# Softmax of batches 4 to 7 with tokens on partitions, turned by DMA both ways

## The chip, the core and the metric

The kernel runs on one core of a Trainium2 chip. The metric is the device time of one execution in microseconds (us). The kernel before takes 241.41 us, the median of three runs (241.13 to 242.18).

## What is computed

Eight batches of eight heads, with 576 tokens of 64 numbers each, go through an attention over 32 memory slots, and the result through a bilinear feed-forward layer:

```python
a = softmax(phi, axis=2)                       # over the tokens
k_m = einsum('bhsm,bhsd->bhmd', a, k)          # 32 memory keys and values per head
v_m = einsum('bhsm,bhsd->bhmd', a, v)
attn = softmax(q @ k_m^T / sqrt(64), axis=-1)  # over the 32 memory slots
x = attn @ v_m                                 # heads side by side: 4608 tokens x 512
out = ((x @ w_a) * (x @ w_b)) @ w_out          # 512 -> 1536 -> 512
```

The change concerns the second softmax: the division of exp(scores) by its sum over the 32 slots.

## The kernel before

For each batch the attention weights lie in a tile with 128 partitions, four heads of 32 memory slots each, and 2 x 576 columns: two groups of heads, tokens along the columns. The memory values are folded into the weights (`vab` = v_m times w_a and w_b), so that the up-projection takes the attention weights `A` directly. A sum over memory slots is thus a sum over partitions, and it is made on TensorE: a product with a block matrix of ones gives each partition the sum of its own head. ScalarE makes 1/sum out of it as exp(-ln(sum)), because both functions lie in one table, and GpSimd (VectorE for batches 0 and 1) multiplies.

```python
def scores(gs):
    if 0 in gs:
        t["E"] = mid.tile([P, 2, S], F16, name="E")           # pool "mid": 2 buffers per name
    if len(gs) > 1 and b > 2:
        work.settle()                                         # gives one PSUM bank back
    ...
        t["pss", g] = [banks.take([P, NI, 32], F32, "pscore", hold=True) for _ in range(2)]
    ...                                                       # 32 small matmuls, 4 banks for both groups

def exp_scores(g):
    Ev = t["E"].rearrange("p g (i z s) -> p g i z s", z=2, s=32)
    for z in range(2):
        pss, bank = t["pss", g][z]
        nc.scalar.activation(out=Ev[:, g, :, z, :], in_=pss, func=AF.Exp, scale=1.0 / (8.0 * CS))
        banks.free(bank)

def denominators(g, hfs=range(2)):
    ...
        pD = banks.tile([P, HALF], F32, name="pD")
        nc.tensor.matmul(pD, ones, t["E"][:, g, sl], start=True, stop=True)
        nc.scalar.activation(out=t["L", g][:, sl], in_=pD, func=AF.Ln)

def normalise(g, hfs=slice(0, 2)):
    if g == 0 and hfs.start == 0:
        attn[b] = mid.tile([P, 2, S], F16, name="A")
    ...
    nc.scalar.activation(out=t["R", g][:, sl], in_=t["L", g][:, sl], func=AF.Exp, scale=-1.0)
    engine = nc.vector if b < 2 else nc.gpsimd
    engine.tensor_tensor(out=attn[b][:, g, sl], in0=t["E"][:, g, sl], in1=t["R", g][:, sl], op=ALU.mult)
```

The fold needs four banks for 512 columns of both weight matrices; ScalarE empties those of group 0 and VectorE those of group 1:

```python
def take_fold(lo, hi, z):
    for g, engine_copy in enumerate((nc.scalar.copy, nc.vector.tensor_copy)):
        pva, bank = t["pva", lo, z][g]
        engine_copy(out=vabs[b][z][:, g, lo:hi], in_=pva[:, 0:hi - lo])
        banks.free(bank)
```

The up-projection of batch b runs in half steps, each two matmuls for `pa` and two for `pb`, of 288 columns. ScalarE copies `pa` to `a_sb`, VectorE multiplies it with `pb` into `ht`:

```python
def up_half(b, i, hf, x):
    ps = banks.tile([P, HALF], F32, name=("pa", "pb")[x])
    for g in range(2):
        nc.tensor.matmul(ps, vabs[b][x][:, g, P * i:P * (i + 1)], attn[b][:, g, HALF * hf:HALF * (hf + 1)], ...)
    if x == 0:
        ...
        nc.scalar.copy(out=a_sbs[b, i, hf], in_=ps)
    else:
        nc.vector.tensor_tensor(out=ht[:, i, t0:t0 + HALF], in0=a_sbs.pop((b, i, hf)), in1=ps, op=ALU.mult)
```

A batch has 24 half steps, and after each there is a slot. In a slot come first the output products that are due (`py`, `pv`, `px`: pairs of token blocks by a seven-product scheme of Strassen's kind, with sums `h_sums` and `w_sums` added up on GpSimd), and then the units that a schedule string names: "sc" the scores, "e0" and "e1" the exponentials of the two groups, "den" the sums, "nr" the division, "v0" to "v2" the fold of 512 columns, "x0a" and so on its copies out, "kv" and "km" the sums of keys and values and their scaling, "kvt" and "kvd" their transposition on TensorE or by DMA, "qt" the transposition of q, "exp" the exponential of phi, "L" the loads of a later batch, "d3" three output products out of turn. A stroke (') means the batch after. The strings `second`, `every` and `last` hold the preparation of batch 3, of batches 4 to 6, and of batch 7.

PSUM has eight banks. `banks.take` hands out the one whose turn is longest ago and that is not held; a matmul into a bank waits until the engine that read it last is done.

The weight sums are additions on GpSimd, issued after batch 1's preparation:

```python
def sum_weights():
    t = [w_sums[:, x] for x in range(4)]
    for out, in0, in1 in (...):                               # 4 sums, each in two halves of 128x768
        for x in range(2):
            ...
            nc.gpsimd.tensor_tensor(out=out[:, sl], in0=in0[:, sl], in1=in1[:, sl], op=ALU.subtract)
```

Of the kernel before, what the change touches and what calls it, by code (L numbers as in the profile page):

```python
# [8 lines left out]
F32 = mybir.dt.float32  # L9
F16 = mybir.dt.float16  # L10
AF = mybir.ActivationFunctionType
ALU = mybir.AluOpType

P = 128
# [4 lines left out]
def kernel(  # L19
# [11 lines left out]
    nc = tc.nc  # L31

    B, H, S, D = q.shape
    M = phi.shape[3]
# [11 lines left out]
    mid = ctx.enter_context(tc.tile_pool(name="mid", bufs=2))  # L46
    small = ctx.enter_context(tc.tile_pool(name="small", bufs=2))
# [130 lines left out]
    attn = {}  # L178
    vabs = {}

    def head(g, j):

        jj = j ^ g
        return jj % 2, 2 * g + jj // 2

    def units(b):

        u = {}
        t = {}
# [133 lines left out]
        def normalise(g, hfs=slice(0, 2)):  # L323
# [6 lines left out]
            engine = nc.vector if b < 2 else nc.gpsimd  # L330
            engine.tensor_tensor(out=attn[b][:, g, sl], in0=t["E"][:, g, sl], in1=t["R", g][:, sl], op=ALU.mult)  # L331

        def fold(lo, hi, zs):
            if b not in vabs:
                vabs[b] = [mid.tile([P, 2, d_ff], F16, name=f"vab{x}") for x in range(2)]
            if len(zs) > 1 and b > 2:
                work.settle()
            for z in zs:
                t["pva", lo, z] = [banks.take([P, 512], F32, "pva", hold=True) for _ in range(2)]
                for j in range(4):  # L340
                    for g in range(2):
                        r, hp = head(g, j)
                        nc.tensor.matmul(  # L343
                            t["pva", lo, z][g][0][32 * j:32 * j + 32, 0:hi - lo],
                            t["kvT"][64 * r:64 * r + 64, 4 + g, M * j:M * j + M],
                            w_sbs[z][64 * r:64 * r + 64, hp, lo:hi],
                            start=True,
                            stop=True,
                            tile_position=(64 * r, 32 * j),
                        )  # L350

        def take_fold(lo, hi, z):
            for g, engine_copy in enumerate((nc.scalar.copy, nc.vector.tensor_copy)):
                pva, bank = t["pva", lo, z][g]
                engine_copy(out=vabs[b][z][:, g, lo:hi], in_=pva[:, 0:hi - lo])  # L355
                banks.free(bank)

        def one(f, *a):
            return lambda: f(*a)

        for z in range(2):
            u[f"exp{z}"] = one(exp_phi, z)
            u[f"ks{z}"] = one(sums, z, 0)
            u[f"kt{z}"] = one(transpose, z, 0)
            u[f"vs{z}"] = one(sums, z, 1)
            u[f"vt{z}"] = one(transpose, z, 1)
            u[f"s{z}"] = one(scores, (z,))
            u[f"e{z}"] = one(exp_scores, z)
            u[f"km{z}"] = one(take_kv, (z,))
            u[f"den{z}"] = one(denominators, z)  # L370
            u[f"nr{z}"] = one(normalise, z)
            for hf in range(2):
                u[f"den{z}{hf}"] = one(denominators, z, (hf,))
                u[f"nr{z}{hf}"] = one(normalise, z, slice(hf, hf + 1))
            for n in range(NCH):
                u[f"v{n}{'ab'[z]}"] = one(fold, 512 * n, 512 * (n + 1), (z,))
                u[f"x{n}{'ab'[z]}"] = one(take_fold, 512 * n, 512 * (n + 1), z)
            for n in range(2):
                u[f"hv{n}{'ab'[z]}"] = one(fold, 256 * n, 256 * (n + 1), (z,))
                u[f"hx{n}{'ab'[z]}"] = one(take_fold, 256 * n, 256 * (n + 1), z)  # L380
        for n in range(NCH):
            u[f"v{n}"] = one(fold, 512 * n, 512 * (n + 1), (0, 1))
# [4 lines left out]
        u["km"] = one(take_kv)  # L387
        u["kvt"] = one(kv_transpose)
        u["kvd"] = one(kv_turn)
        u["-"] = lambda: None  # L390
        return u

# [36 lines left out]
    w_sums = wpool.tile([P, 4, KH, NH], F16, name="w_sums")  # L429

    def quarter(x, y):
        return wo_sb[:, KH * x:KH * (x + 1), NH * y:NH * (y + 1)]

    def sum_weights():
        t = [w_sums[:, x] for x in range(4)]
        for out, in0, in1 in ((t[0], quarter(0, 1), quarter(0, 0)), (t[1], quarter(1, 1), t[0]),
                              (t[2], quarter(1, 1), quarter(0, 1)), (t[3], quarter(1, 0), t[1])):
            for x in range(2):
                sl = slice(KH // 2 * x, KH // 2 * (x + 1))
                nc.gpsimd.tensor_tensor(out=out[:, sl], in0=in0[:, sl], in1=in1[:, sl], op=ALU.subtract)  # L440
# [182 lines left out]
    def ups(steps, side=()):  # L623

        side = iter(side)
        for step in steps:
            for _ in up(*step):
                work.advance()
                next(side, us[step[0]]["-"])()
        for f in side:  # L630
            work.advance()
            f()
# [5 lines left out]
    def half_steps(b, hf, lo=0):  # L638

        return [(b, i, (hf,)) for i in range(lo, NFF)]  # L640

    us = {b: units(b) for b in range(B)}

    def named(b, names):
# [6 lines left out]
    def slots(b, names):  # L651

        def both(fs):
            return lambda: [f() for f in fs]
        def unit(n):
            if n == "fin":
                return lambda: work.pull(-work.done % NFF)
            if n == "L":
                return lambda: load(b + 2) if b + 2 < B else None
            if n[0] == "y":  # L660
                return lambda: some(int(n[1:]))
            if n[0] == "d" and n[1:].isdigit():
                return lambda: work.pull(int(n[1:]))
            return us[b + n.endswith("'") - n.endswith("_")][n.rstrip("'_")]

        return [both([unit(n) for n in x.split("+")]) for x in names.split()]
# [26 lines left out]
    chain(1, "exp0 y3 exp1 y8 ks0 y1 qt0 y2 kt0 y2 qt1 s0 ks1 y3 e0 y1 kt1 qt2 y1 qt3 den0 y3 s1 y1 nr0 y4 vs0 e1 vs1 y1 den1 y2 vt0 vt1 nr1 y2 hv0a hx0a hv0b y1 hx0b y2")  # L693
    load(3)
    sum_weights()
    ups(steps(1, 0, 4), slots(1, "- y1+hv1a+hx1a hv1b+hx1b - y3+v1a+x1a y3+v1b+x1b - -"))
    ups(half_steps(1, 0, 4), slots(1, "- v2a+x2a+v2b+x2b+qt0' - - qt1'+exp0' exp1'+qt2' - kv'+km'+y9"))
    work.plan(S + HALF, 10)
    ups(half_steps(1, 1, 4), slots(2, "qt3 kvt - sc+e0+e1 - den0+den1+nr0 - v0+nr1+x0a x0b - v1+x1b x1a"))
    second = "v2_+d1+x2a_+exp0 x2b_ exp1 - kv+km+d2 qt0 d4+kvt+qt1 - qt2+qt3+sc+e0 - e1+v0+d2+x0a+x0b den0+d3 exp0' v1+nr0+x1a x1b+qt0' L+d5 den1 v2+x2a exp1'+qt1'+x2b - - qt2'+kv'+nr1+km' - - qt3'+kvt'+d5"  # L700
    every = "- sc+e0 e1 den0 nr0+v0+x0a+x0b - - exp0' exp1' - v1+x1b+x1a+kv'+km0'+d3 - den1+km1' kvd'+qt0' - - nr1+qt1' v2+x2a+x2b - qt2' - qt3' - - L"
    last = "sc+e0 d3 - e1 v0+x0b - - den1 - - den0+d1 x0a+v1+x1b x1a+nr0 - - - v2+x2a - nr1 - - - - x2b"
    for b in range(2, B):
        if b == 2:
            load(4)
# [35 lines left out]
```

The softmax here doesn't subtract the row's maximum and nothing guards it: scores larger than these inputs give would overflow.

## Time and profile before

| | of the profiled execution |
|---|---|
| span | 239.6 us |
| mean granted TensorE clock | 0.997 |
| matmuls of the sums (pD), count and listed mean | 32, 286 ns |
| ln on ScalarE (L), count and mean | 32 of 128x288, 418 ns |
| exp(-ln) on ScalarE (R), count and mean | 14 of 128x576, 702 ns; 4 of 128x288, 441 ns |
| multiplication on GpSimd (A), count and mean | 12 of 128x576, 1278 ns |
| key/value transposition by DMA (kvT), count and time to landing | 3, median 3.3 us |

The profile lists busy time for each engine; PE is TensorE's matmuls and PEld its weight loads, DVE is VectorE, ACT is ScalarE, POOL is GpSimd, SP issues DMAs. Matmuls overlap in the pipeline, so that the listed length of one is longer than the time it takes away from the next; the distance between two starts tells that time. In a view by stretches there stand, after the stretch, its length, then for each of PE, PEld, DVE, ACT and POOL the busy time with the number of instructions, then the clock, the DMA share and GB/s. In a view by order of time there stand the start, the length, the engine, the line, the operation, its tiles (out<-in) and shapes, and in brackets the idle time before it and what ended it.

### The profile page before, as it was taken

To read this page: it belongs to the slowest core of one execution; us is meant where nothing else is said; L and a number is where in the kernel's file an instruction comes from. 1 tells how busy PE (TensorE), PEld (TensorE's weight loads), DVE (VectorE), ACT (ScalarE), POOL (GpSimd) and SP (SyncE) were. 2 spreads that over 40 slices of the span, in tenths; PEclk is the share of its full clock that TensorE was granted. 3 is DMA by queue.
4 is the path that set the end of the run, shared out by engine and by line. 5 is a ranking of instruction groups with operands and counts; after the bars stand their busy time and mean duration, and the time that the engine had idled before them with its cause. 6 is when DMAs were issued, how large, how long until landed. Compare 5 with 4: busy or idle time off the path is not lost.

```text
span 239.6 us, 7764 instructions
## 1 busy us (share of the span) xinstructions
PE 230.6 (96%) x3092; PEld 170.3 (71%) x3092; DVE 165.4 (69%) x403; ACT 158.7 (66%) x410; POOL 159.5 (67%) x135
## 2 busy tenths in 40 slices
PE   7958999999999999999999999999999999999993
PEld 7734664456757867878787787878787778888882
DVE  4636784469949878966975659775976585756642
ACT  2266671669698599687776867797776877465330
POOL 7953244499979629981799948984769087937001
PEclk9999999999999999999999999999999999999998
DMA  6999999999967954992359945599130303032155
GB/s 230 239 197 207 206 258 206 252 213 279 224 154 161 214 115 98 222 208 49 43 123 233 211 90 65 141 212 191 41 85 11 81 16 74 10 83 61 38 130 125
DMA packets 28164, 34.71 MB, mean 145 GB/s; under 512 B 4416, under 2 KB 22208, under 8 KB 28128
## 3 DMA queue, kind: packets, MB, share of 16 engines
q0 software_dynamic: 19264, 23.14, 52.2%
q1 hardware_dynamic: 8352, 10.29, 18.4%
q10 hardware_dynamic: 512, 0.79, 1.0%
q8 instruction: 24, 0.39, 0.7%
q14 instruction: 12, 0.10, 0.1%
HBM read 42.47 MB, written 9.44 MB: 217 GB/s over the span
## 4 chain that ended last, share of the span: by engine, by line
PE 77%; DMA 16%; DVE 2%; issue 1%; POOL 1%; ACT 1%; DVEq 0%; POOLq 0%
PE py L473 18%; PE pa L601 18%; PE pb L601 17%; PE pv L473 9%; DMA wb_sb<-in_moe_w_b_dram 6%; DMA q_sb<-in_q_dram 5%; PE pva L343 5%; DMA kv_sb<-in_v_dram 4%; PE px L473 4%; PE po L398 2%; PE pkv L212 2%; PE pscore L297 1%; PE pD L320 1%; DVE ht L612 1%; ACT a_sb L609 1%
## 5 line engine op out<-in xcount | busy, mean ns | idle before, releaser
L612 DVE TENSOR_TENSOR ht<-a_sb,pb 128x288 f16<-128x288 f16 x168 | 73.3, 450 | 37.5 <-ACT a_sb L609 26.8
L601 PEld LDWEIGHTS <-vab 128*128 128x128 f16 x768 | 72.4, 98 | 24.9 <-issue 7.8
L609 ACT CAST a_sb<-pa 128x288 f16<-128x288 f32 x168 | 66.7, 407 | 25.7 <-PE pa L601 24.6
L601 PE MATMUL pa<-A,vab 128*128 128x288 f16 x384 | 75.8, 287 | 0.1
L601 PE MATMUL pb<-A,vab 128*128 128x288 f16 x384 | 75.0, 286 | 0.7 <-ACT vab L355 0.5
L455 POOL TENSOR_TENSOR h_sums<-ht 128x768 f16<-128x768 f16 x28 | 46.0, 1644 | 33.9 <-DVE ht L612 33.7
L473 PEld LDWEIGHTS <-h_sums 128*128 128x128 f16 x384 | 37.0, 98 | 7.7 <-issue 1.1
L355 DVE CAST vab<-pva 128x512 f16<-128x512 f32 (+1 forms) x52 | 32.3, 644 | 4.8 <-PE pva L343 4.2
L355 ACT CAST vab<-pva 128x512 f16<-128x512 f32 (+1 forms) x52 | 27.7, 569 | 7.8 <-PE pva L343 7.2
L473 PEld LDWEIGHTS <-ht 128*128 128x128 f16 x288 | 28.1, 98 | 5.7 <-issue 0.4
L473 PE MATMUL py<-w_sums,h_sums 128*128 128x256 f16 x192 | 31.3, 273 | 0.0
L455 POOL TENSOR_TENSOR h_sums<-h_sums,ht 128x768 f16<-128x768 f16 x14 | 23.0, 1640 | 1.0
L455 POOL TENSOR_TENSOR h_sums<-ht,h_sums 128x768 f16<-128x768 f16 x14 | 23.0, 1642 | 0.9
L310 ACT ACTIVATE E<-pscore 128x288 f16<-128x288 f32 x32 | 11.4, 419 | 11.4 <-PE pscore L297 11.2
L331 POOL TENSOR_TENSOR A<-E,R 128x576 f16<-128x576 f16 x12 | 15.3, 1278 | 4.3 <-ACT R L329 4.3
L473 PE MATMUL py<-wo_sb,ht 128*128 128x256 f16 x96 | 16.7, 273 | 0.0
L473 PE MATMUL pv<-w_sums,h_sums 128*128 128x256 f16 x96 | 16.5, 273 | 0.0
L473 PE MATMUL py<-w_sums,ht 128*128 128x256 f16 x96 | 15.9, 272 | 0.1
L473 PE MATMUL px<-wo_sb,ht 128*128 128x256 f16 x96 | 15.9, 273 | 0.0
L321 ACT ACTIVATE L<-pD 128x288 f32<-128x288 f32 x32 | 11.5, 418 | 6.0 <-PE pD L320 5.8
L480 ACT ACTIVATE u<-py 128x256 f32<-128x256 f32 x32 | 12.5, 390 | 4.3 <-PE py L473 3.7
L203 DVE STREAM_TRANSPOSE qT<-q_sb 128x288 f32<-128x288 f32 x32 | 14.6, 464 | 0.3 <-DMA q_sb<-in_q_dram 0.3
(65 smaller groups left out, 275.7 us busy)
## 6 DMA issues: line engine op xcount, KB each, us to landing
out_dram<-o_sb SPq DMA_DIRECT2D x68, 128.0 KB, 2.4
phi_sb<-in_phi_dram POOLq DMA_DIRECT2D x8, 576.0 KB, 5.4
kv_sb<-in_v_dram POOLq DMA_DIRECT2D x7, 576.0 KB, 10.3
kv_sb<-in_k_dram POOLq DMA_DIRECT2D x7, 576.0 KB, 6.6
q_sb<-in_q_dram POOLq DMA_DIRECT2D x6, 576.0 KB, 13.1
wo_sb<-in_moe_w_out_dram POOLq DMA_DIRECT2D x6, 256.0 KB, 13.7
q_sb<-in_q_dram POOLq DMA_DIRECT2D x4, 288.0 KB, 9.7
wa_sb<-in_moe_w_a_dram POOLq DMA_DIRECT2D x2, 512.0 KB, 13.8
```

The costliest lines, as they stand in the source:

```text
L203: nc.vector.transpose(out=t["qT"][:, hp, :].bitcast(F32), in_=qs[b][:, hp, :].bitcast(F32))
L310: nc.scalar.activation(out=Ev[:, g, :, z, :], in_=pss, func=AF.Exp, scale=1.0 / (8.0 * CS))
L321: nc.scalar.activation(out=t["L", g][:, sl], in_=pD, func=AF.Ln)
L331: engine.tensor_tensor(out=attn[b][:, g, sl], in0=t["E"][:, g, sl], in1=t["R", g][:, sl], op=ALU.mult)
L343: nc.tensor.matmul(t["pva", lo, z][g][0][32 * j:32 * j + 32, 0:hi - lo], t["kvT"][64 * r:64 * r + 64, 4 + g, M * j:M * j + M], w_sbs[z][64 ...
L355: engine_copy(out=vabs[b][z][:, g, lo:hi], in_=pva[:, 0:hi - lo])
L455: engine.tensor_tensor(out=out, in0=in0, in1=in1, op=op)
L473: nc.tensor.matmul(po, lhs[:, i], rhs[:, i], start=first and i == 0, stop=i == KH - 1, skip_group_check=not first)
L480: nc.scalar.mul(out=x, in_=po, mul=scale)
L601: nc.tensor.matmul(ps, vabs[b][x][:, g, P * i:P * (i + 1)], attn[b][:, g, HALF * hf:HALF * (hf + 1)], start=(g == 0), stop=(g == 1))
L609: nc.scalar.copy(out=a_sbs[b, i, hf], in_=ps)
L612: nc.vector.tensor_tensor(out=ht[:, i, t0:t0 + HALF], in0=a_sbs.pop((b, i, hf)), in1=ps, op=ALU.mult)
```

## The change

For batches 4 to 7 the exponentials E are transposed by a DMA into a tile ET with tokens on the partitions: nine blocks of 128x128. There, the 32 memory slots of a head lie side by side in one partition, so VectorE can sum them with tensor_reduce, take the reciprocal of the sums, and the division is one multiplication with the reciprocal broadcast over 32 columns, five blocks of it on GpSimd and four on VectorE. A second DMA turns the result back into A. The product with ones, the ln and the exp(-ln) are not needed for these batches. Two of the fold's twelve copies of a batch move from VectorE to ScalarE in exchange (columns 512 to 1023, group 1, batches 4 to 7). The schedules of batch 3 on are rewritten, with the loads of later batches earlier, and batch 4's key/value transposition goes by DMA. GpSimd's weight additions are held behind batch 1's division by a copy of one column that reads its result.

```diff
+        def e_turn():
+            t["ET"] = mid.tile([P, 2, S], F16, name="E").rearrange("p g s -> p (g s)").rearrange("p (n x) -> p n x", x=P)
+            nc.sync.dma_start_transpose(out=t["ET"], in_=t["E"].rearrange("p g s -> p (g s)"))
+
+        def blocks(x):
+            return t["ET"][:, slice(0, 5) if x == 0 else slice(5, 9)].rearrange("p n (j m) -> p (n j) m", m=M)
+
+        def token_sums(x):
+            if x == 0:
+                t["sum"] = small.tile([P, 36], F32, name="sum")
+            out = t["sum"][:, slice(0, 20) if x == 0 else slice(20, 36)]
+            nc.vector.tensor_reduce(out=out, in_=blocks(x), axis=mybir.AxisListType.X, op=ALU.add)
+            nc.vector.reciprocal(out=out, in_=out)
+
+        def token_normalise(x):
+            sums = t["sum"][:, slice(0, 20) if x == 0 else slice(20, 36)]
+            engine = (nc.gpsimd, nc.vector)[x]
+            engine.tensor_tensor(out=blocks(x), in0=blocks(x), in1=sums.unsqueeze(2).to_broadcast(list(blocks(x).shape)),
+                                 op=ALU.mult)
+
+        def a_turn():
+            attn[b] = mid.tile([P, 2, S], F16, name="A")
+            nc.sync.dma_start_transpose(out=attn[b].rearrange("p g s -> p (g s)").rearrange("p (n x) -> p n x", x=P),
+                                        in_=t["ET"].rearrange("p n x -> p (n x)"))
...
-            for g, engine_copy in enumerate((nc.scalar.copy, nc.vector.tensor_copy)):
+            copies = (nc.scalar.copy, nc.scalar.copy if b > 3 and lo == 512 else nc.vector.tensor_copy)
+            for g, engine_copy in enumerate(copies):
...                       # "ed" is e_turn, "sm0" "sm1" token_sums, "tn0" "tn1" token_normalise, "ad" a_turn
     def sum_weights():
+        nc.gpsimd.tensor_copy(out=w_sums[:, 0, 0, 0:1], in_=attn[1][:, 1, S - 1:S])
...
-    second = "v2_+d1+x2a_+exp0 x2b_ exp1 - kv+km+d2 qt0 d4+kvt+qt1 - qt2+qt3+sc+e0 - e1+v0+d2+x0a+x0b den0+d3 exp0' v1+nr0+x1a x1b+qt0' L+d5 den1 v2+x2a exp1'+qt1'+x2b - - qt2'+kv'+nr1+km' - - qt3'+kvt'+d5"
-    every = "- sc+e0 e1 den0 nr0+v0+x0a+x0b - - exp0' exp1' - v1+x1b+x1a+kv'+km0'+d3 - den1+km1' kvd'+qt0' - - nr1+qt1' v2+x2a+x2b - qt2' - qt3' - - L"
-    last = "sc+e0 d3 - e1 v0+x0b - - den1 - - den0+d1 x0a+v1+x1b x1a+nr0 - - - v2+x2a - nr1 - - - - x2b"
+    second = "v2_+d2+x2a_+x2b_+exp0 - exp1 - kv+km+d2 qt0 d4+qt1+kvt qt2 L+d1+qt3+sc+e0 - d2+v0+e1+x0a+x0b - den0+exp0'+d2 v1+nr0+x1a x1b+d10+exp1' - qt0' v2+x2a+x2b+kv' - den1+km0' km1'+kvd' nr1+qt1' qt2' qt3' - d6"
+    every = "exp0' sc+exp1'+e0+d3+e1+v0+x0a+x0b+ed - kv'+km0' km1' - d4+sm0 sm1+tn0+kvd' - tn1+d2 d3 v1+qt0'+x1a+ad d3+L+x1b qt1' - qt2' - v2+x2a+x2b - qt3' - - - - -"
+    last = "sc e0+e1+ed - v0+x0b - - sm0 x0a+sm1+tn0 d2+v1+d3+x1b+tn1 - ad+d6 x1a - - - - v2+x2a - - - - - x2b"
```

More of the change, by code (lines that the diff above doesn't have):

```diff
@@ L389, in units @@
         u["kvd"] = one(kv_turn)
+        u["ed"] = e_turn
+        for x in range(2):
+            u[f"sm{x}"] = one(token_sums, x)
+            u[f"tn{x}"] = one(token_normalise, x)
+        u["ad"] = a_turn
         u["-"] = lambda: None
```

## The prediction, made before the changed kernel ran

> **What bounds the kernel now.** I read the page's busy times first, then TensorE's own waits, then four 20 us stretches, then the order of time on TensorE. The page and the stretches:
>
> ```profile
> PE 230.6 (96%) x3092; PEld 170.3 (71%) x3092; DVE 165.4 (69%) x403; ACT 158.7 (66%) x410; POOL 159.5 (67%) x135
> ...
> 60.00:80.00 20.00, 19.74 (x348) 13.86 (x346) 15.76 (x41) 15.88 (x42) 18.03 (x14) 1.00 0.89 182
> 100.00:120.00 20.00, 20.00 (x298) 15.19 (x297) 16.07 (x40) 15.44 (x41) 12.73 (x9) 1.00 0.62 111
> 160.00:180.00 20.00, 20.00 (x288) 15.71 (x285) 16.15 (x40) 15.28 (x39) 13.04 (x9) 1.00 0.56 113
> ```
>
> TensorE is busy all of the time from about 100 us on, while VectorE stands at 16.1 of 20 us, ScalarE at 15.4 and GpSimd at 12.7. A busy PE could still hide bubbles, because matmuls overlap, so I look at distances between starts:
>
> ```profile
> 157.47 0.49 PE L473 MATMUL px<-wo_sb,ht 128*128 128x256 f16 x3
> 157.80 0.41 PE L320 MATMUL pD<-E,ones 128*128 128x288 f16 x2
> 158.04 0.41 PE L601 MATMUL pa<-A,vab 128*128 128x288 f16 x2
> ```
>
> Three matmuls of 256 columns take 0.33 us from start to start, 0.11 each; two of 288 columns take 0.24 to 0.245 us, 0.1225 each. This pace is held through the batches from 100 us on, without a hole, apart from about 0.2 us at each change between full matmuls and those on small tiles. So in that part a microsecond is won only by taking matmuls away from TensorE, and lost by whatever makes it wait. The waits that TensorE did have are early: the view of waits by engine names six of them, the longest 1.3 us, and none is in the steady part. The end is TensorE too: after the last up-projection, only output products remain.
>
> **What the Trainium skill says.** "Perfetto Trace Analysis", section "Identifying the Most-Contended Engine", says that matmul busy time is no measure of how full TensorE is; the trace agrees (the page lists 286 ns for a pD matmul whose slot is 122). "TensorE: Matmul & The Clock Gate", section "Back-to-back issue gap", gives N/2.4 + 2.5 ns as an isolated warm gap, 122.5 ns for 288 columns; the distances above agree. "VectorE: DVE Perf Modes", section "The perf-mode tier table", holds tensor_reduce to one element per cycle, whatever the type. No tensor_reduce is in this trace. "SBUF — State Buffer", section "Who interferes with whom", says that a VectorE instruction with two SBUF inputs and a GpSimd instruction that reads SBUF shut each other out for a whole instruction. The profile shows no such pair meeting in the place that the change guards: batch 1's last division on VectorE runs from 47.37 to 47.83 us, and GpSimd's first weight addition starts at 48.74.
>
> **The change, part by part.**
>
> Taken from TensorE: four pD matmuls in each of batches 4 to 7, 16 x 0.1225 = **1.96 us**. The new schedule also turns batch 4's key and value matrices by DMA (kvd' stands where kvt' stood), which removes six transposes on TensorE; a group of six takes
>
> ```profile
> 99.47 0.50 PE L241 MATMUL pT<-ident,rep 128*128 128x128 f16 x6
> 99.80 0.60 PE L473 MATMUL pv<-wo_sb,h_sums 128*128 128x256 f16 x4
> ```
>
> 99.80 - 99.47 = **0.33 us**. The instruction lists of the two programs differ by these 22 matmuls. Together 2.29 us, all on the engine that sets the end.
>
> ScalarE, per batch: four Ln go (0.30 each from start to start, so 1.2), two Exp(-L) go (105.22 to 105.81, so 0.59 each, 1.18), and two casts of 128x512 come over from VectorE (0.94 for two). Net -1.4 us.
>
> VectorE, per batch: two casts leave (1.28 for a pair). Two tensor_reduce of 640 and 512 elements, two reciprocals (0.16 each as in the row of rphi) and one multiply of 512 elements come in. By ht's full-rate row (288 elements, 450 ns alone) and the 684 ns of a 512 cast, I estimate 0.82, 0.68 and 0.69 us for the three; with the reciprocals 2.5. Net +1.2 us of about 24, so VectorE goes from 80% to 85%. It stays below TensorE.
>
> GpSimd, per batch: two multiplies of 576 (1278 ns each) go, one of 640 comes; at 1278/576 = 2.22 ns an element, 1.42 us. Net -1.1 us.
>
> The two turns: each moves nine blocks of 128x128. The key/value turn of six blocks lands in 2.7 to 3.7 us, median 3.3; for nine I estimate 4.0 to 5.5 us. The first must land before sm0 on VectorE, in slot 6; the scores are in slot 1. Let S be the time at which the scores' matmuls are over. E is complete at about S + 1.45 (below), so ET lands near S + 5.9. The slots between hold five pairs of up-products (2.45), the sums of keys and values (0.87), twelve output products (1.3) and the fold (1.0), so TensorE passes sm0's place at S + 5.6, and VectorE, which runs some 0.8 us behind, at S + 6.4. About half a microsecond to spare. The second turn is issued around slot 11 and is needed in slot 24: 12 us of room for some 5. Off the path.
>
> The held weight additions: one copy of 128x1 on GpSimd, behind an instruction that ended 0.9 us before the additions began anyway. Zero in this profile; it guards against a meeting that didn't occur here.
>
> **What takes some of it back.** The new order puts scores, both exponentials and the fold v0 into one slot. There are eight PSUM banks: the scores hold four, one is held by the open output product, so the fold must wait for banks that ScalarE is still reading. The kernel before has this once, where batch 3's second exponential and v0 share a slot:
>
> ```profile
> 85.27 0.46 PE L343 MATMUL pva<-wa_sb,kvT 64*32 64x512 f16 x8
> 85.30 0.82 DVE L612 TENSOR_TENSOR ht<-a_sb,pb 128x288 f16<-128x288 f16 x2 [0.94 <-ACT a_sb L609]
> 85.44 0.76 ACT L310 ACTIVATE E<-pscore 128x288 f16<-128x288 f32 x2
> 85.81 0.41 PE L343 MATMUL pva<-wb_sb,kvT 64*32 64x512 f16 x8
> ```
>
> 0.54 us between the two halves of the fold, against 0.22 in the steady batches: 0.3 us lost. In the new order I follow ScalarE: four E at 0.30 from S + 0.09 (last one written at S + 1.41), then x0a and x0b at 0.47 each, written at about S + 1.9 and S + 2.4. TensorE wants those banks earlier: the second pair after the scores at S + 1.7, and the key sums at S + 2.2. I get 0.2 + 0.25 = 0.45 us a batch, for batches 4, 5 and 6 (the last schedule spreads these out), 1.35 us in all. The margins are tens of nanoseconds and any output scaling between them moves them, so I count half, **0.7 us**.
>
> Sum: 241.4 - 2.3 + 0.7 = **239.8 us**. For the reshuffled schedule between batches 2 and 3 I count nothing: it can lose or regain a wait of 0.3 us like the one above.
>
> **The rivals.**
> First, **VectorE becomes the wait**. For: in slots 1 to 9 of batch 4 it gets nine ht (0.37 us each from start to start), two casts (0.64), both key/value scalings (1.7 for the two), the reduces with reciprocals (1.7), tn1 (0.7) and three output sums (1.1), 9.8 us of work, while TensorE needs 8.7: nine pairs of up-products (4.4), scores (0.4), fold (0.6), sums (0.9), 22 output products (2.4). VectorE falls about 1 us behind there. Besides, tn1 has two SBUF inputs and may stand behind a GpSimd addition of 1.64 us, and sm0 waits in order for a transfer. Against: six banks rotate under the up-products, three slots or 2.5 us, of which VectorE's usual lag takes 0.8, and the later slots are light. If so, about 0.5 to 1 us more per batch for four batches: 241 to 243 us.
> Second, **the waits of slot 1 do not arise**, because ScalarE has lost its Ln and Exp(-L) and is ahead; then the full 2.3 us remain and the smoother middle part gives another 0.5 to 1: 238.2 to 239.1 us.
> Third, **the turns are slow** beside loads and stores (the one at 145.7 us took 3.7 us beside stores): a landing after 7 us stops VectorE about 1 us a batch, of which the banks hide most. 240.5 to 242 us.
> A larger gain would need TensorE time that the change doesn't free, and a larger loss a stop of over 2 us a batch.
>
> **Range and chances.** The sure part is 2.3 us off. Full losses of the first rival give 242, the second rival 238. I take **239.8 us, with 237.6 to 241.9** for eight times in ten. Two per cent is 4.8 us, 236.6 or 246.2; neither sum gets there. Faster by over 2%: 0.05; within 2%: 0.92; slower by over 2%: 0.03.
>
> **What would show it.** In the profile after: 16 pD matmuls instead of 32 and 3070 matmuls instead of 3092; the distance of scores from batch to batch 0.5 us shorter, less what slot 1 gives back; a longer distance than 0.22 us from the first half of v0 to the second; ET landing in under 5.5 us; the reduces near 0.8 and 0.7 us; the weight additions still starting near 49 us. I would be wrong if TensorE shows waits on VectorE in slots 6 to 12, if the new A lands late for its first product, or if the part before 100 us moves by more than 1 us, of which I count none.

## The result, and the profile after

The changed kernel takes 239.57 us (239.41 to 239.74), the kernel before 241.32 us in the same runs: a ratio of 0.992, with an interval of 0.990 to 0.995. It is 0.8% faster, and the prediction was 239.8.

From the page of the kernel after, the busy times:

```profile
PE 228.5 (96%) x3070; PEld 168.0 (71%) x3070; DVE 169.1 (71%) x414; ACT 153.1 (64%) x394; POOL 154.9 (65%) x132
```

From its stretches, two of the three of before (length, then busy time of PE, PEld, DVE, ACT, POOL; the last three columns are the granted clock, the DMA share and GB/s):

```profile
100.00:120.00 20.00, 19.97 (x293) 14.65 (x292) 16.95 (x44) 15.40 (x39) 14.81 (x12) 1.00 0.56 120
160.00:180.00 20.00, 20.00 (x223) 15.48 (x222) 15.99 (x40) 14.04 (x37) 10.07 (x7) 1.00 0.43 80
```

TensorE is still the engine that decides, with 22 matmuls fewer. ScalarE and GpSimd gave up 5.6 and 4.6 us over the whole execution and VectorE took on 3.7, and none of that moved the end (e1, below, keeps all that work and is as fast). The new instructions, from the groups of the kernel after with shapes kept apart:

```profile
L350 POOL TENSOR_TENSOR E<-E,sum 128x640 f16<-128x640 f16 x4 | 5.1, 1263 | 10.6 <-DVE sum L345 10.6
L320 PE MATMUL pD<-E,ones 128*128 128x288 f16 x16 | 3.4, 286 | 0.7 <-ACT E L310 0.6
L350 DVE TENSOR_TENSOR E<-E,sum 128x512 f16<-128x512 f16 x4 | 3.4, 858 | 0.0
L344 DVE TENSOR_REDUCE sum<-E 128x20 f32<-128x640 f16 x4 | 3.2, 812 | 0.0
L344 DVE TENSOR_REDUCE sum<-E 128x16 f32<-128x512 f16 x4 | 2.7, 674 | 0.0
L345 DVE RECIPROCAL sum<-sum 128x20 f32<-128x20 f32 x4 | 1.1, 278 | 0.1
```

The turns, from its view of DMAs (issues, median us to landing); ET bears the name E there, because it shares E's buffers:

```profile
kvT<-rep SPq DMA_TRANSPOSE x4, 2.9
E<-E SPq DMA_TRANSPOSE x4, 3.5
A<-E SPq DMA_TRANSPOSE x4, 3.2
```

Slot 1 of batch 3, in the order of time on TensorE: scores, three output products, the fold v0, two half steps, and the beginning of the sums of keys and values:

```profile
101.76 0.47 PE L297 MATMUL pscore<-qT,kvT 32*32 32x288 f16 x32
102.17 0.50 PE L505 MATMUL py<-w_sums,ht 128*128 128x256 f16 x3
102.60 0.41 PE L368 MATMUL pva<-wa_sb,kvT 64*32 64x512 f16 x8
102.82 0.40 PE L368 MATMUL pva<-wb_sb,kvT 64*32 64x512 f16 x8
103.16 0.42 PE L633 MATMUL pa<-A,vab 128*128 128x288 f16 x2
103.41 0.41 PE L633 MATMUL pb<-A,vab 128*128 128x288 f16 x2
103.66 0.41 PE L633 MATMUL pa<-A,vab 128*128 128x288 f16 x2
104.10 0.40 PE L633 MATMUL pb<-A,vab 128*128 128x288 f16 x2
104.43 0.81 PE L212 MATMUL pkv<-kv_sb,exp_sb 64*32 64x192 f16 x45
```

The halves of v0 stand 0.22 us apart, so the fold itself did not wait. The wait comes later: from the last pa to the last pb are 0.44 us instead of 0.245.

Where the 1.9 us between the two profiled spans came from is seen in the first up-product of each batch, before and after: batch 3 at 100.35 and 99.92, batch 4 at 124.48 and 123.78, batch 5 at 153.91 and 152.76, batch 6 at 178.59 and 177.36, batch 7 at 202.28 and 200.46, end at 239.6 and 237.7. A batch's stretch runs from its first up-product to that of the next batch. The stretches in which matmuls were removed are shorter, by 0.3, 0.3, 0.45, 0.1 and 0.6 us from batch 2 on; they do not all contain the same output products, and they hold losses too (below). The first 72 us and the tail are alike within 0.12 us.

### The profile page after: what moved, and what is told of

It is laid out like the page before. It is cut to its first block, busy times and chain, and to the rows that moved or that the text cites. A ratio compares the mean times of both kernels' runs of the same rounds, so it can differ in the third digit from the quotient of the medians.

```text
span 237.7 us, 7733 instructions
## 1 busy us (share of the span) xinstructions
PE 228.5 (96%) x3070; PEld 168.0 (71%) x3070; DVE 169.1 (71%) x414; ACT 153.1 (64%) x394; POOL 154.9 (65%) x132
## 4 chain that ended last, share of the span: by engine, by line
PE 90%; DMA 3%; ACT 2%; DVE 2%; issue 2%; DVEq 0%; POOLq 0%
PE pa L633 21%; PE pb L633 20%; PE py L505 18%; PE pv L505 9%; PE pva L368 6%; PE po L429 5%; PE px L505 4%; DMA phi_sb<-in_phi_dram 3%; PE pkv L212 2%; PE pscore L297 2%; PE pk L260 1%; PE pw L151 1%; DVE ht L644 1%; PE pD L320 1%; ACT L L321 1%
## 5 line engine op out<-in xcount | busy, mean ns | idle before, releaser
L644 DVE TENSOR_TENSOR ht<-a_sb,pb 128x288 f16<-128x288 f16 x168 | 72.0, 446 | 33.2 <-ACT a_sb L641 24.6
L641 ACT CAST a_sb<-pa 128x288 f16<-128x288 f32 x168 | 65.7, 410 | 31.3 <-PE pa L633 28.1
L381 ACT CAST vab<-pva 128x512 f16<-128x512 f32 (+1 forms) x60 | 31.9, 579 | 7.3 <-PE pva L368 7.0
L381 DVE CAST vab<-pva 128x512 f16<-128x512 f32 (+1 forms) x44 | 26.9, 637 | 5.7 <-PE pva L368 5.7
L505 PE MATMUL py<-w_sums,h_sums 128*128 128x256 f16 x192 | 30.5, 273 | 0.0
L310 ACT ACTIVATE E<-pscore 128x288 f16<-128x288 f32 x32 | 10.9, 417 | 9.0 <-PE pscore L297 8.8
L505 PE MATMUL pv<-w_sums,h_sums 128*128 128x256 f16 x96 | 15.7, 273 | 0.0
L505 PE MATMUL py<-wo_sb,ht 128*128 128x256 f16 x96 | 15.7, 273 | 0.0
L505 PE MATMUL px<-wo_sb,ht 128*128 128x256 f16 x96 | 15.2, 273 | 0.0
L505 PE MATMUL pv<-wo_sb,h_sums 128*128 128x256 f16 x96 | 14.4, 273 | 0.0
L194 ACT ACTIVATE exp_sb<-phi_sb 128x576 f16<-128x576 f32 x16 | 10.8, 689 | 5.4 <-DMA phi_sb<-in_phi_dram 5.4
## 6 DMA issues: line engine op xcount, KB each, us to landing
kv_sb<-in_v_dram POOLq DMA_DIRECT2D x7, 576.0 KB, 11.8
```

What stands on the lines that cost most here:

```text
L194: nc.scalar.activation(out=t["exp"][:, 2 * z:2 * z + 2, :, :], in_=phis[b][:, 2 * z:2 * z + 2, :].rearrange("p c (i m) -> p c i m", m=M), ...
L505: nc.tensor.matmul(po, lhs[:, i], rhs[:, i], start=first and i == 0, stop=i == KH - 1, skip_group_check=not first)
```

## The experiments

The theory: TensorE's time decides, so the removed matmuls are the gain, and everything else is hidden or a small loss. The rivals: the new order and the lighter engines made the gain; or VectorE and the turns stand close behind and set a limit of their own.

**e1, the matmuls alone.** In the kernel before, ln reads E instead of the sums. This kernel leaves the sum over memory slots out in batches 4 to 7, so its output there is not a softmax.

```diff
-                pD = banks.tile([P, HALF], F32, name="pD")
-                nc.tensor.matmul(pD, ones, t["E"][:, g, sl], start=True, stop=True)
+                if b > 3:
+                    pD = t["E"][:, g, sl]
+                else:
+                    (as before)
```

> The kernel before, with the product of E and the ones left out in batches 4 to 7: ln reads E itself, so the division is not a softmax there. Nothing else moves. If TensorE's time decides, 16 matmuls of 0.1225 us go and the time falls by 1.96 us, from 241.3 to 239.4. If the gain of the changed kernel comes from the new order of units or from the lighter ScalarE, little happens here: 241.0 to 241.4.

239.67 us, ratio 0.993 (0.992 to 0.995). The old order with all its work on ScalarE, VectorE and GpSimd, but without the 16 matmuls, is as fast as the changed kernel. What the change gains is these matmuls; what its six removed transposes add, its new order takes back.

**e2, the matmuls put back** into the changed kernel, read by nobody.

```diff
                 t["sum"] = small.tile([P, 36], F32, name="sum")
+                pD = banks.tile([P, HALF], F32, name="pD")
+                for g in range(2):
+                    for hf in range(2):
+                        nc.tensor.matmul(pD, ones, t["E"][:, g, HALF * hf:HALF * (hf + 1)], start=True, stop=True)
```

> The changed kernel with four matmuls of E and ones put back per batch 4 to 7, ahead of the sums on VectorE; nobody reads their result. If TensorE's time decides: 239.6 + 1.96 = 241.5 us, the old time. If the gain comes from the order of units or from the other engines' relief: 239.6 to 240.2 us.

241.57 us, ratio 1.0006 (0.9995 to 1.0018): the old time again. By the first up-products the stretches of batches 3 to 6 are longer than in the changed kernel by 0.49, 0.54, 0.48 and 0.49 us, which is four times 0.1225 each. Removing and restoring agree with the 1.96 us of the arithmetic, one with 1.6 and the other with 2.0 us. The rival that the order or the relief of the other engines made the gain falls.

**e3, without the hold.**

```diff
-        nc.gpsimd.tensor_copy(out=w_sums[:, 0, 0, 0:1], in_=attn[1][:, 1, S - 1:S])
```

> The changed kernel without the copy that holds the weight additions. In the profile before, the additions began 0.9 us after the division's end without any hold, so I expect the same time, 239.6 within 0.2 us. If the hold matters, the additions start earlier, meet the division on VectorE and cost up to one addition, 1.6 us: 240 to 241 us.

239.59 us. In its trace VectorE's division of batch 1 runs from 47.21 to 47.67 and the first addition starts at 48.60. GpSimd issues a load of q just ahead of the additions, and that issue starts at 47.84, after 0.55 us of idle time that the view puts down to this division. So the additions come late without the copy, and the hold has nothing to hold in these executions.

```profile
47.84 0.74 POOL L90 DMA_DIRECT2D q_sb<-in_q_dram  x1 [0.55 <-DVE A L331]
48.60 1.65 POOL L471 TENSOR_TENSOR w_sums<-wo_sb 128x768 f16<-128x768 f16 x1
```

**e4 and e9, batch 4's key and value turn on TensorE**, once in the slot of its scaling and once three slots later:

```diff
-km1'+kvd' nr1+qt1' qt2' qt3' - d6
+km1'+kvt' nr1+qt1' qt2' qt3' - d6        # e4
+km1' nr1+qt1' qt2' qt3' kvt' d6          # e9
```

> The changed kernel with batch 4's key and value matrices turned by six TensorE transposes again, where the DMA turn stood. If TensorE's time decides, 0.33 us more: 239.9 us. If that turn is worth nothing: 239.6 us.

> The changed kernel with batch 4's key and value matrices turned on TensorE, three slots after their scaling instead of in its slot, so that TensorE finds them ready. If the turn is worth only TensorE's time for six transposes: 239.6 + 0.33 = 239.9 us. If putting it on TensorE costs more than its matmuls wherever it stands: 241 us or more.

e4 takes 241.53 us, e9 239.99 us (ratios 1.001 and 0.994). TensorE in e4, in order of time:

```profile
96.59 0.28 PE L241 MATMUL pT<-ident,rep 128*128 128x128 f16 x2
97.94 0.49 PE L241 MATMUL pT<-ident,rep 128*128 128x128 f16 x4 [1.06 <-DVE rep L233]
```

My first edit had built a new wait: TensorE stood 1.06 us for the scaled keys, and the two groups of transposes start 1.35 us apart. Batch 2's stretch is 1.89 us longer than in the changed kernel. Without the wait (e9), that stretch is 28.13 us long against 27.79, 0.34 more, which is the predicted value of six transposes. The profiled execution of e9 is 1.5 us longer as a whole, but 0.96 us of that lie ahead of batch 2, where the two programs are the same.

**e5, key and value sums behind the scores.**

```diff
-exp0' sc+exp1'+e0+d3+e1+v0+x0a+x0b+ed - kv'+km0' km1' -
+exp0'+exp1' sc+kv'+e0+d3+e1+v0+x0a+x0b+ed - km0' km1' -
```

> The changed kernel with the next batch's sums of keys and values placed right behind the scores in slot 1, instead of in slot 3 by themselves, and both exponentials of phi in slot 0. Two things should go: the wait for PSUM banks two half steps after the fold (0.2 us in two of three batches), since ScalarE gets 0.9 us more to empty the scores' banks, and one change between full and small tiles per batch (about 0.25 us). If both are real, 0.2 to 1.2 us less: 238.4 to 239.4, I take 238.7. If the changes between tile shapes cost nothing and the wait only moves: 239.6 us.

242.76 us, ratio 1.007 (1.004 to 1.009): slower than both, and my expectation was wrong. TensorE in the order of time:

```profile
155.61 0.47 PE L297 MATMUL pscore<-qT,kvT 32*32 32x288 f16 x32
157.44 0.77 PE L212 MATMUL pkv<-kv_sb,exp_sb 64*32 64x192 f16 x56 [1.36 <-ACT E L310]
```

The view puts the 1.36 us down to ScalarE's E, but TensorE needs no result of E here, and in the program these sums stand ahead of the exponentials. The values of that batch were issued at 145.8 and landed at 157.3 us, just before pkv starts at 157.44; in the batch before, a shorter wait at the same place is put down to that load. The slot where "kv'" stood was the slot where its data had arrived. Nor did the wait that this run was to remove go away: the second half step behind the fold now waits 0.3 us in each of three batches, instead of 0.2 us in two.

**e6, the two casts back on VectorE.**

```diff
-            copies = (nc.scalar.copy, nc.scalar.copy if b > 3 and lo == 512 else nc.vector.tensor_copy)
+            copies = (nc.scalar.copy, nc.vector.tensor_copy)
```

> The changed kernel with the fold's copies as before, two casts per batch back on VectorE (1.28 us a batch). If VectorE has slack behind its banks: 239.6 within 0.3 us. If VectorE is close to deciding the time: 0.5 us or more a batch, 241.5 us.

239.63 us. The casts fall into slots 11 and 12, where 1.3 us more on VectorE are hidden; its busy time between 100 and 120 us is 18.1 of 20 us there.

**e7 and e8, more work and a later turn for VectorE** in slots 6 and 7: each tensor_reduce done twice, and the first turn issued twice.

```diff
+            nc.vector.tensor_reduce(out=t["sum2"][:, slice(0, 20) if x == 0 else slice(20, 36)], in_=blocks(x),
+                                    axis=mybir.AxisListType.X, op=ALU.add)             # e7
+            for _ in range(2):                                                         # e8
+                nc.sync.dma_start_transpose(out=t["ET"], in_=t["E"].rearrange("p g s -> p (g s)"))
```

> The changed kernel with each tensor_reduce done twice, the first into a tile that nobody reads: 1.5 us more VectorE work per batch 4 to 7, in slots 6 and 7. If the six rotating banks cover it: under 0.4 us more in all, 239.6 to 240.0. If VectorE is what TensorE waits for in these slots, most of 4 x 1.5 us comes through: 243 us or more.

> The changed kernel with the first turn (E to ET) issued twice, the second waiting for the first, so that ET is complete about 3.3 us later, 1.8 us after VectorE wants it. If the banks cover a VectorE stop of that length: under 0.5 us more in all, 239.6 to 240.1. If a late turn comes through: about 1 us a batch, 243 us.

e7 takes 242.63 us, 3.1 more than the changed kernel, half of the 5.9 us that it adds to VectorE. e8 takes 247.1 us, 7.5 more: the median of five executions between 245.7 and 248.9 us, without a sixth that fell into a slower state. From e7 the place where TensorE stops, in order of time, and from e8 a line of the waits:

```profile
111.44 0.41 PE L637 MATMUL pa<-A,vab 128*128 128x288 f16 x2
112.54 0.41 PE L637 MATMUL pb<-A,vab 128*128 128x288 f16 x2 [0.69 <-DVE ht L648]
```

```profile
DVE sum L345 <- DMA E<-E: 8.8, 4, 3.0
```

In the profiled execution of e8 VectorE stands 8.8 us in four waits for ET, and the span is 9.3 us longer than that of the changed kernel. So VectorE in slots 6 and 7 has little room, and most of a late turn comes through. That the two numbers are so close is partly chance: behind the longest stop of TensorE, 2.2 us, the granted clock is 0.5 from 170.9 to 174.3 us, which takes away about 1.7 us besides the stops (an estimate: half of the 3.4 us). Slots 11 and 12 of e6 and slots 6 and 7 of e7 are different places: VectorE has slack in one and not in the other.

**e10, the new softmax in the old order of units**, and **e12, the same with the loads four slots earlier.**

```diff
-every = "exp0' sc+exp1'+e0+d3+e1+v0+x0a+x0b+ed - kv'+km0' km1' - d4+sm0 sm1+tn0+kvd' - tn1+d2 d3 v1+qt0'+x1a+ad d3+L+x1b qt1' ..."
+every = "- sc+e0 e1+ed - v0+x0a+x0b - - sm0+exp0' sm1+tn0+exp1' tn1 v1+x1b+x1a+kv'+km0'+d3 ad km1' kvd'+qt0'+L ..."     # e10
+every = "- sc+e0 e1+ed - v0+x0a+x0b - - sm0+exp0' sm1+tn0+exp1' tn1+L v1+x1b+x1a+kv'+km0'+d3 ad km1' kvd'+qt0' ..."     # e12
```

> The changed softmax for batches 4 to 6 in the order of units of the kernel before: scores and exponentials over two slots, the fold v0 two slots later, and the sums of keys and values right behind the fold v1, so that they share a change of tile shape. If the crowded slot 1 and the extra change of tile shape cost what the gaps say (0.2 us for the waits in two of three batches, 0.1 to 0.3 us per batch for the change): 239.6 - 0.4 to 1.2, I take 238.9 us. If the new order is what makes room for the turns: VectorE waits for ET or TensorE for A, and the time is 240 us or more.

> The kernel of e10_old_order with one thing moved: the loads of a later batch are issued in slot 9, behind the first half of the division, instead of in slot 13. In e10 the loads began some 4 us later than in the changed kernel, and the first turn of the next batch, going out beside them, took 7.4 and 7.8 us instead of 3.2 to 4.2. If that is what e10 lost, the turns are short again and the time is 239.2 us, between 238.7 and 239.6, which is at or below the changed kernel. If the order of units itself was at fault (the sums of keys and values behind the fold waiting for VectorE's banks), it stays at 241.5 us or more.

243.16 us (ratio 1.010, 1.006 to 1.013) and 244.47 us (ratio 1.012, 1.010 to 1.014). Both expectations failed. The turns in the views of DMAs, first e10, then e12:

```profile
E<-E SPq DMA_TRANSPOSE x4, 5.3
```

```profile
kvT<-rep SPq DMA_TRANSPOSE x4, 7.3
E<-E SPq DMA_TRANSPOSE x4, 3.4
A<-E SPq DMA_TRANSPOSE x4, 6.9
```

In e10 the loads began at 118.2 us and were still moving when ET was to be filled: its turns took 7.8 and 7.4 us in two batches. VectorE waited for them, and TensorE's fold and key sums waited for VectorE:

```profile
DVE sum L344 <- DMA E<-E: 4.2, 2, 2.9
PE pva L368 <- DVE ht L644: 1.5, 2, 0.8
PE pkv L212 <- DVE ht L644: 1.2, 2, 0.6
```

In e12 the loads began beside the turn of A. Issues of GpSimd and SP in e12, in order of time:

```profile
110.21 0.81 POOL L78 DMA_DIRECT2D phi_sb<-in_phi_dram  x1
...
111.10 1.95 SPq L355 DMA_TRANSPOSE A<-E  x1
...
112.49 0.75 POOL L90 DMA_DIRECT2D q_sb<-in_q_dram  x1
```

That turn landed at 124.28, after 13.2 us, and the key/value turns behind the loads took 11.8 and 12.7 us. TensorE waited for both, as the waits of e12 say:

```profile
PE pscore L297 <- DMA kvT<-rep: 2.8, 1, 2.8
...
PE pa L633 <- DMA A<-E: 0.6, 1, 0.6
```

Behind the stop of 2.8 us the granted clock is 0.5 for 3.4 us, so that matmuls take double their time there: this stop costs more than its length.

e12 did repair what it was built to repair: E's turns are down to a median of 3.4 us, and the waits of the fold and of the key sums for VectorE are gone. It moved the loss to the other turns. In the changed kernel the turns of E and A touch only the ends of the loads, as its issues on GpSimd show:

```profile
112.80 1.64 POOL L487 TENSOR_TENSOR h_sums<-ht 128x768 f16<-128x768 f16 x1 [1.87 <-DVE ht L644]
114.38 0.81 POOL L78 DMA_DIRECT2D phi_sb<-in_phi_dram  x1
```

A is turned from 112.1 to 115.3 us, the loads begin at 114.4 and end at 129.5, and the next E goes out at 128.3. By these traces the place of the loads, which I had read as a detail of the schedule, is what keeps the turns short; no run moved the loads alone in the changed kernel.

**e11, batch 3 as well.**

```diff
-d2+v0+e1+x0a+x0b - den0+exp0'+d2 v1+nr0+x1a x1b+d10+exp1' - qt0' v2+x2a+x2b+kv' - den1+km0' km1'+kvd' nr1+qt1'
+d2+v0+e1+x0a+x0b+ed - exp0'+d2 v1+x1a x1b+d10+exp1' sm0 sm1+tn0 tn1+v2+x2a+x2b+kv' ad km0' km1'+kvd' qt0'+qt1'
```

> The changed kernel with batch 3 divided in the same way (its sums, ln and exp(-ln) go; E and A turned by DMA inside the order of batch 2). If only TensorE's time counts: four more pD matmuls go, 239.6 - 0.5 = 239.1 us. If the chain of turn, sums, division and turn doesn't fit between the scores in slot 8 and the first use in slot 24: TensorE waits for A of batch 3 and the time is 240 us or more.

250.73 us, ratio 1.037 (1.035 to 1.040). TensorE and VectorE in it, from the order of time and the waits:

```profile
92.89 0.40 PE L368 MATMUL pva<-wb_sb,kvT 64*32 64x512 f16 x8
101.69 0.67 PE L212 MATMUL pkv<-kv_sb,exp_sb 64*32 64x192 f16 x20 [8.41 <-DVE ht L644]
```

```profile
DVE sum L344 <- DMA E<-E: 7.9, 2, 7.6
```

E of batch 3 was turned at 86.4 us, in the middle of the loads issued from 82.2 us on (the last landed at 101.0). The turn's last packets went out at 99.5, VectorE started the sum at 100.2, and TensorE stood 8.4 us behind it. When TensorE went on, the granted clock was 0.5 until 107.5 us, as this stretch shows (the column before the last two):

```profile
103.40:107.60 4.20, 4.20 (x19) 2.73 (x18) 3.56 (x11) 1.58 (x4) 0.00 (x0) 0.51 0.37 70
```

The stop and the slow stretch behind it make up the 10.9 us by which batch 2's stretch is longer than in the changed kernel. In batch 2's schedule the loads lie on the place of the turn; whether batch 3 would gain with its loads elsewhere, no run tried.

No version that computes the reference was faster than the changed kernel.

## Why the prediction was right, and where it was not

**The sum's first term held.** 1.96 us for 16 matmuls and 0.33 us for six transposes: e1, e2 and e9 measured 1.6, 2.0 and 0.34 to 0.42.

**The second term had nearly the right size, but other parts.** I counted 0.7 us for waits in slot 1, and nothing for the new order between batches 2 and 3. The fold's halves were to stand further apart than 0.22 us; they do not. The wait at the second half step after it came, 0.2 us in two of three batches, 0.4 in all. The wait before the key sums did not come: the 0.09 us there stand ahead of every group on small tiles, in both kernels (so in slot 1 above the three output products ahead of the fold take 0.43 us and need 0.33). The larger part I had left out. In the kernel before, the key sums stood right behind the fold v1 and shared its change between small and full tiles:

```profile
165.83 0.41 PE L343 MATMUL pva<-wa_sb,kvT 64*32 64x512 f16 x8
166.06 0.40 PE L343 MATMUL pva<-wb_sb,kvT 64*32 64x512 f16 x8
166.27 0.95 PE L212 MATMUL pkv<-kv_sb,exp_sb 64*32 64x192 f16 x72
167.15 0.50 PE L473 MATMUL py<-w_sums,h_sums 128*128 128x256 f16 x3
```

In the changed kernel, in the same stretch of batch 5, each stands by itself:

```profile
157.07 0.60 PE L505 MATMUL px<-wo_sb,ht 128*128 128x256 f16 x4
157.60 0.94 PE L212 MATMUL pkv<-kv_sb,exp_sb 64*32 64x192 f16 x72
158.48 0.30 PE L633 MATMUL pa<-A,vab 128*128 128x288 f16 x1
...
165.99 0.41 PE L368 MATMUL pva<-wa_sb,kvT 64*32 64x512 f16 x8
166.22 0.40 PE L368 MATMUL pva<-wb_sb,kvT 64*32 64x512 f16 x8
166.55 0.42 PE L633 MATMUL pa<-A,vab 128*128 128x288 f16 x2
```

Together they took 1.32 us from the first start to the next full matmul. Apart they take 0.56 and 0.88, and 0.09 more ahead of the key sums (0.53 us for four output products that need 0.44): 1.53. So the extra change costs 0.2 us a batch, 0.6 in the stretches of batches 3 to 5. Against these losses of 1.0 us stand gains that I had not counted either: in batch 2's stretch the wait between the halves of a fold is 0.2 us shorter and one change of tile shape is gone (0.2 us), and in batch 4's stretch a wait of 0.15 us is gone. What is left is about 0.5 us, close to the 0.7 that I took; that the parts came out so is luck.

**The estimates of single operations** were close: 0.82 and 0.68 us for the sums, measured 0.81 and 0.67; 1.42 for GpSimd's multiplication, measured 1.26. The reciprocals cost 0.28 and 0.25 instead of 0.16, because the row they came from has one element. The turns landed in 3.2 to 4.2 us for E, mostly under the 4.0 to 5.5 of the estimate: with nothing beside them, six blocks took 2.8 us and nine took 3.2, so most of a turn's time doesn't grow with the blocks.

**The first rival** did not come true in the changed kernel, but its working was off on both sides. The parts of VectorE's 9.8 us add up to 9.2, so that VectorE would have fallen 0.5 us behind and not 1. And I gave VectorE 1.7 us of cover from the rotating banks (2.5 less 0.8); in e7, of 1.5 us more per batch, 1.1, 0.8, 0.8 and 0.4 us came through in the four batches, so that only 0.4 to 1.1 us were left.

**The third rival** did not come true either; by e10 and e12 that hangs on the place of the loads, which the prediction did not see. I wrote "12 us of room for some 5" for the second turn and called it off the path; in e12 it took 13.2 us and was on the path. I had judged a slow turn to be mostly hidden; e8 shows that it isn't.

**The hold** is worth nothing here (e3), as the profile before had said. That the two instructions would hinder each other if they met is shown at another place, below.

## What to carry to other kernels

Where TensorE is full by the distances between starts, price a change by the matmuls it takes away, and try that price alone first: leaving out the matmuls shows nearly the whole gain in one run, and it needs no new softmax. A DMA transposition can take several times its short time while much of large loads is still to come, so place loads and turns one after the other, and read the landing time of each turn, not their median. A stop of TensorE of 2 us or more cost more than its length in three runs here, so read the granted clock behind it. An engine's share of busy time does not tell its slack: the same 1.3 to 1.5 us on VectorE cost nothing in one slot and half its length in another.

## What the runs showed of the hardware

A transposition by DMA of nine 128x128 blocks lands in 3.2 us alone and, in e10 and e12, in 7.4 to 13.2 us beside loads of 576 KB; six blocks in 2.8 us alone and in 11.8 to 12.7 us beside them. Not every overlap costs as much: in the changed kernel the E turned at 156.3 us landed after 4.2 us, with the last load in flight until 159.6. Loads are not the only cause either: one turn of six blocks took 5.6 us there after the loads had ended.

Behind the longest stops TensorE's granted clock is 0.5 for some microseconds: from 97.3 to 107.5 us in e11 (a stop of 8.4 us until 101.7), from 158.1 to 161.6 in e12 (2.8 us until 158.2), and from 170.9 to 174.3 in e8 (2.2 us until 169.5). Behind the stops of 1.06 us in e4 and 1.36 us in e5 it stays at 1.0.

VectorE's multiplication of ET with the broadcast sums, both inputs in SBUF, takes 0.68 us in three batches and 1.38 us in the fourth. From the order of time after, the batch where GpSimd was adding, VectorE second:

```profile
137.88 1.63 POOL L487 TENSOR_TENSOR h_sums<-ht,h_sums 128x768 f16<-128x768 f16 x1
```

```profile
138.69 1.38 DVE L350 TENSOR_TENSOR E<-E,sum 128x512 f16<-128x512 f16 x1
```

It ends 0.56 us after GpSimd's addition does, as if most of it had run only then. GpSimd's next addition, issued beside it at 139.48, took 2.09 us instead of 1.64. In the other three batches GpSimd was idle. This agrees with the Trainium skill, "SBUF — State Buffer", section "Who interferes with whom": a VectorE instruction with two SBUF inputs and a GpSimd instruction that reads SBUF shut each other out.
